# adaLN attention, mixer and MLP on one core: matmul order in the MLP and in attention, PSUM pools, and the hand-over to mixing

## The chip, the cores and the metric

The kernel runs on one core of a Trainium2 chip. The metric is the device time of one execution in microseconds. The kernel before was timed three times: 1797.48, 1798.19 and 1798.49 us, median 1798.19. One further execution was profiled; it took 1793.53 us, and the trace, its page and all rows quoted below are of that one.

Engines are named as the profile names them: PE (matmuls; PEld is its weight load, which runs beside them), DVE (vector), ACT (scalar), POOL (GpSimd) and SP, whose queue issues nearly all DMAs. L12 is line 12 of the kernel.

## What is computed

One transformer block over 2048 rows of 576 features, with three stages. The conditioning vector c gives six vectors (sa, ca, ga, sb, cb, gb) by silu(c) times w_mod.

```
h  = layernorm(x) * (1 + ca) + sa
x  = x + ga * (attention(h) @ wo)             # 32 heads of 18, causal window of 256 rows
h  = layernorm(x) * (1 + cb) + sb
g  = gelu(layernorm(h) @ w1)                  # 576 x 576
x1 = h + shift(g) @ w2                        # four feature groups, shifted by +1, -1, +2, -2 rows
h2 = gelu(layernorm(x1) @ w3) @ w4            # 576 -> 4608 -> 576
x  = x + gb * (x1 + h2)
```

All of it is in 32-bit floats. The kernel splits each operand into a high and a low part that PE can multiply fast, and adds three products (high x high, high x low, low x high) in PSUM: a contraction over 576 features takes 14 matmuls, namely 3 for each of four chunks of 128, and 2 for the tail of 64.

## The kernel before

Rows are cut into 16 tiles of 128 and four blocks of 512; a block is the moving operand of most matmuls. Three phases follow each other.

**Attention** (`phase_a`, L161). It works through 32 units u, eight per row block: a unit is four heads of one row block. For a unit, `pack` (L431) loads Q and K from DRAM, where the Q and K products had been stored; `scores` (L446) makes 16 score tiles "sc" and takes each row's maximum on DVE; `attend` (L494) recomputes the transposed scores X in three PSUM banks for each head (L504), adds masks by matmuls with an identity (L513), takes the exponential on ACT (`ex`), multiplies by V (`av`, L534), transposes and divides (`ot`, `on`), and stores the result to `od` in DRAM (L555). The table `banks` (L491) lists, bank by bank, the pieces of X as (key tile, first query tile, width in tiles, place in the bank); `low` (L492) the masks as (which, place, width). Between these, the Q, K and V products of the next row block are played: `x_tr` (L328) transposes the normalized rows in five chunks k (PE, then ACT to a 32-bit buffer h, then POOL's high and DVE's low part) into the tile hT, and `qk_item` and `v_item` (L370, L412) are its 17 products of 14 matmuls. The window of a row block for these products, in units, is in `win` (L700). When the last window is over, `s4a` (L703) does the output product, the residual, the two norms and the modulation for the first 12 row tiles, beside the last attention units; it stores rows to DRAM as xp, hbd and xnd.

**Mixing** (`phase_b`, L923). Rows come back from xnd, are transposed (`split9`, L67: four 128-wide transposes "pa" and a tail "pb" per row tile, a high part by ACT, L74 and L80, and a low part by DVE, L75 and L81) into tiles xnT of 512 rows, and go through W1 (`w1c`, products pg, L986) and gelu into G; shifted, they go through W2 (L1037). The last four row tiles of the output product (`s4`) run here too. `w2t` (L936) loads the 64 rows of W2 that make its tail chunk, splits them and moves the low part by DMA.

**MLP** (`phase_c`, L1168). 36 units: two halves of the rows (blk) times 18 pairs of 128 hidden features (fg). In a unit, `up` makes four items of 14 matmuls 128x512 (L1231) with a gelu each; POOL and ACT and DVE form sums and splits of the results (`after`, L1211). `down` takes a unit's results one unit later: seven combinations m times four row tiles i are 28 groups of three matmuls 128x288 (L1276), and each is added to an accumulator in SBUF by DVE (L1283). The seven combinations replace eight products of 2 x 2 blocks.

**What sets the order.** Every step is put on a list with a time number, in units, and `play` (L42) sorts the list: the numbers are no times on the chip, they are the order of the program. In attention and MLP the engines then run their instructions in that order; mixing is ordered by the framework's own scheduler. A step that needs a buffer waits until its last reader is done. PSUM has eight banks: in attention 3 "sc" (scores), 2 "st" (X), and one each of "tr" (transposes), "av" and "mm" (products); in the other phases 3 "w1", 2 "w2", 2 "tr" and one "mm", from a pool of its own. In SBUF, "L" is one buffer that holds hT in turn, then 8 rows of `s4a` (s4rows), then xnT0, xnT3 and LNT3; "L2" has three for the other xnT and LNT tiles.

Lines of importance for what follows: the spread of the parts of an up item, L1237, and the time of a down group, L1321.

```
ev += spread([part(2 * k, 2 * k + 2) for k in range(7)], t, t + 0.25)      # L1237
t = t0 + 0.005 + 0.965 * (n + 0.5) / 28                                    # L1321
```

## Time and profile before

| what | us |
|---|---|
| timed, median of 3 | 1798.19 |
| profiled execution | 1793.53 |
| its span, first to last instruction | 1791.7 |
| start and first products | 0 to 66 |
| attention with products | 66 to 507 |
| attention with `s4a` | 507 to 707 |
| between attention and mixing | 707 to 722 |
| mixing | 722 to about 890 |
| MLP | about 890 to 1791 |

The stages were read off the trace: attention's last copy stands at 707.05 and the first mixing product at 722.13. A row of busy time by stage has the window, its length, and for each engine the busy microseconds and the instructions; then the granted clock of PE as a share of full speed, the busy share of the DMA engines, and GB/s. A timeline row has start, duration, engine, line, operation, output and inputs, shape of the stationary and moving operands, and how many such instructions in a row; in brackets, the time that the engine had stood idle and what ended that. Matmuls overlap, so a row's duration is longer than the distance to the next row's start; what a group costs PE is that distance. A row of a waits view has who waited, for what, how many microseconds in all, how often, and the longest.

### The profile page before, as it was taken

To read this page: it belongs to the slowest core of one execution; us is meant where nothing else is said; L and a number is where in the kernel's file an instruction comes from. 1 tells how busy PE (TensorE), PEld (TensorE's weight loads), DVE (VectorE), ACT (ScalarE), POOL (GpSimd) and SP (SyncE) were. 2 spreads that over 40 slices of the span, in tenths; PEclk is the share of its full clock that TensorE was granted. 3 is DMA by queue.
4 is the path that set the end of the run, shared out by engine and by line. 5 is a ranking of instruction groups with operands and counts; after the bars stand their busy time and mean duration, and the time that the engine had idled before them with its cause. 6 is when DMAs were issued, how large, how long until landed. Compare 5 with 4: busy or idle time off the path is not lost.

```text
span 1791.7 us, 31913 instructions
## 1 busy us (share of the span) xinstructions
PE 1712.6 (96%) x11100; PEld 1431.1 (80%) x11100; DVE 1227.2 (68%) x3050; ACT 713.7 (40%) x1310; POOL 839.5 (47%) x829
## 2 busy tenths in 40 slices
PE   8899999999988897999999999999999999999998
PEld 5767777777866675788988888888888888888887
DVE  3564665575566764676777778887777777777777
ACT  3354454464455555444243344443332222222221
POOL 7332332321135553011188888888875333333335
PEclk9999999999999999899999999999999999999999
DMA  7554454434356654543455565556655444444442
GB/s 214 165 161 139 126 160 133 116 116 119 105 120 179 205 152 134 170 129 108 139 196 179 202 213 199 188 187 204 208 203 191 141 149 145 161 140 164 141 133 90
DMA packets 161544, 283.41 MB, mean 158 GB/s; under 512 B 38756, under 2 KB 77668, under 8 KB 161384
## 3 DMA queue, kind: packets, MB, share of 16 engines
q1 hardware_dynamic: 161064, 280.85, 49.3%
q8 instruction: 88, 1.44, 0.3%
q14 instruction: 72, 0.59, 0.1%
q10 hardware_dynamic: 320, 0.52, 0.1%
HBM read 168.86 MB, written 111.78 MB: 157 GB/s over the span
## 4 chain that ended last, share of the span: by engine, by line
PE 75%; DVE 7%; POOL 6%; DMA 5%; issue 4%; ACT 2%; SPq 1%; DVEq 0%; POOLq 0%; ACTq 0%
PE p L1231 21%; PE p L1276 19%; PE qk L365 6%; PE av L534 4%; PE X L504 4%; PE sc L457 4%; PE v L365 3%; PE X L513 3%; PE w L1037 2%; PE pg L986 2%; PE po L752 2%; DMA r<-in_B_w_dram 1%; POOL g L1204 1%; POOL c L1132 1%; DMA wm<-in_w_mod_dram 1%
## 5 line engine op out<-in xcount | busy, mean ns | idle before, releaser
L1231 PE MATMUL p<-LNT,W 128*128 128x512 f32 x2016 | 628.7, 399 | 0.0
L1276 PEld LDWEIGHTS p<-W,G 128*128 128x128 f32 x3036 | 505.2, 189 | 116.7 <-DVE accA L1283 14.7
L1276 PE MATMUL p<-W,G 128*128 128x288 f32 x3036 | 559.9, 296 | 16.7 <-DVE accA L1283 7.7
L464 DVE CUSTOM_DVE_ANT_0 sc<-sc,mask 128x384 f32<-128x384 f32 (+2 forms) x512 | 271.4, 542 | 199.7 <-PE sc L457 197.3
L1283 DVE TENSOR_TENSOR accA<-p,accA 128x288 f32<-128x288 f32 x672 | 293.1, 453 | 134.9 <-PE p L1276 131.9
L1231 PEld LDWEIGHTS p<-LNT,W 128*128 128x128 f32 x2016 | 327.4, 188 | 5.4
L1204 POOL TENSOR_TENSOR g<-g,g 128x512 f32<-128x512 f32 x140 | 204.9, 1463 | 245.6 <-ACT g L1235 240.3
L523 ACT ACTIVATE P<-X 128x512 f32<-128x512 f32 (+2 forms) x384 | 216.8, 570 | 230.7 <-PE X L513 224.9
L1199 DVE TENSOR_TENSOR G<-g,G 128x512 fp32r<-128x512 f32 x249 | 247.1, 992 | 28.2 <-ACT G L1196 27.7
L1196 ACT CAST G<-g 128x512 fp32r<-128x512 f32 x249 | 154.7, 621 | 225.5 <-POOL g L1204 222.0
L1235 ACT ACTIVATE g<-p 128x512 f32<-128x512 f32 x144 | 85.7, 595 | 360.3 <-DVE accA L1283 211.3
L457 PE MATMUL sc<-K,Q 108*128 108x384 f32 (+2 forms) x512 | 191.1, 381 | 6.1 <-DMA k0d<-qe 2.7
L504 PE MATMUL X<-Q,K 110*128 110x128 f32 (+2 forms) x704 | 163.1, 306 | 4.4 <-ACT P L523 3.8
L365 PE MATMUL qk<-hT,Wc 128*128 128x512 f32 x504 | 160.3, 417 | 2.7 <-ACT qe L386 1.3
L504 PEld LDWEIGHTS X<-Q,K 110*128 110x128 f32 x704 | 123.6, 191 | 30.0 <-issue 9.5
L390 POOL CAST qe<-qe 128x512 fp32r<-128x512 f32 x36 | 22.1, 615 | 255.8 <-ACT qe L386 245.7
L1283 DVE TENSOR_TENSOR accB<-p,accB 128x288 f32<-128x288 f32 x268 | 114.0, 448 | 26.9 <-PE p L1276 24.9
L513 PE MATMUL X<-maskb,identb 128*128 128x256 bf16 (+1 forms) x640 | 120.5, 254 | 0.0
L457 PEld LDWEIGHTS sc<-K,Q 108*128 108x128 f32 x512 | 96.9, 192 | 28.5 <-issue 11.8
L365 PEld LDWEIGHTS qk<-hT,Wc 128*128 128x128 f32 x504 | 87.7, 194 | 17.6 <-issue 5.1
L534 PE MATMUL av<-P,V 128*32 128x384 f32 (+2 forms) x1408 | 99.6, 395 | 0.0
L365 PE MATMUL v<-Wv,hT 128*128 128x288 f32 x448 | 82.9, 307 | 3.8 <-ACT qe L386 2.9
(902 smaller groups left out, 2087.1 us busy)
## 6 DMA issues: line engine op xcount, KB each, us to landing
w4d<-W SPq DMA_DIRECT2D x55, 576.0 KB
W<-w4d SPq DMA_DIRECT2D x55, 576.0 KB
w3d<-W SPq DMA_DIRECT2D x36, 640.0 KB
W<-w3d SPq DMA_DIRECT2D x36, 640.0 KB
K<-k0d SPq DMA_DIRECT2D x96, 108.0 KB
r<-in_B_w_dram SPq DMA_DIRECT2D x36, 288.0 KB
Q<-q0d SPq DMA_DIRECT2D x128, 72.0 KB
K<-k1d SPq DMA_DIRECT2D x48, 108.0 KB
```

The lines of the kernel that those rows point to most:

```text
L365: nc.tensor.matmul(pm, pl()[i][0], pl()[i][1], start=(i == 0), stop=(i == 13))
L457: nc.tensor.matmul(sc[:, lo:], q[0:2 * R3, h, i * P:(i + 1) * P], k[0:2 * R3, h // 2, i * P + lo:(i + 3) * P], start=True, stop=True)
L464: nc.vector.tensor_tensor_reduce(out=sc[:, lo:], in0=sc[:, lo:], in1=mask[:, lo:], scale=1.0, scalar=-3e38, op0=ALU.add, op1=ALU.max, accu ...
L504: nc.tensor.matmul(x[:, p0 * P:(p0 + w) * P], k[0:2 * R3 + 2, h // 2, (kb + 2) * P:(kb + 3) * P], q[0:2 * R3 + 2, h, q0 * P:(q0 + w) * P], ...
L513: nc.tensor.matmul(x[:, p0 * P:(p0 + w) * P], self.identb, m, start=False, stop=(n == len(ms) - 1))
L523: nc.scalar.activation(pt[:, c0:c1, h % 2, :], x[:, c0 * P:c1 * P].rearrange("p (a b) -> p a b", b=P), AF.Exp, scale=SCALE)
L534: nc.tensor.matmul(abox[0][32 * h:32 * h + 32, q0 * P:(q0 + w) * P], v[:, hh * VA:hh * VA + 32], Pt[b, h // 2][:, p0:p0 + w, h % 2, :], st ...
L1199: nc.vector.tensor_tensor(out=sp[m][:, 1], in0=src(), in1=sp[m][:, 0].bitcast(F32), op=sub)
L1204: nc.gpsimd.tensor_tensor(out=g[o] if o in g else gt(o), in0=g[a], in1=g[b], op=op)
L1231: nc.tensor.matmul(box["p"], box["l"][i][1], box["l"][i][0], start=(i == 0), stop=(i == 13))
L1276: nc.tensor.matmul(po, a, b, start=(n == 0), stop=(n == len(seq) - 1))
L1283: nc.vector.tensor_tensor(out=acc[m, i], in0=po, in1=acc[m, i], op=ALU.add)
```

## The change

Seven edits, which move, add and resize steps; no matmul, cast or transfer is taken away.

1. **MLP order.** The 14 matmuls of an up item are played as two runs of seven, where they were seven pairs. The down groups stand in bursts of three or four between these runs, where they were spread evenly.
2. **One PSUM pool** "ps" for all phases, with the attention's tags: "w1" is taken from the three "sc" banks, "w2" from the two "st" banks, and the transposes of mixing and half of the down groups ("t2") take "tr" and "av" in turn.
3. **Mixing's first tiles.** Only LNT0 still uses the buffer "L"; xnT0, xnT3 and LNT3 go to "L2". V, Q and K get a pool of their own. The first four row tiles are transposed in the "w1" and "w2" banks. `w2t` is placed at 0.2, after the first mixing steps, where it stood at -0.9.
4. **Order in an attention bank.** Bank 0 begins with its 384-wide piece, and its masks are in the other order.
5. **Prologue.** The first weights' loads are issued after the conditioning step: a 1x1 memset on DVE stands ahead of them. Some of the first products take the "av" bank in place of "mm", and the fourth Q/K product is a little earlier.
6. **Row blocks.** The five chunks of `x_tr` follow each other at 0.08 units from 0.4 before the window, where it was 0.16 from 0.8 before. Their 32-bit buffer is a pair of two in "qe". The windows in `win` are longer.
7. **Tail of attention.** Tiles of `s4a` start at 0.75 + 0.70 t after the window, where it was 0.85 + 0.72 t, and take the tile "oT" later.

The diff, cut to its core:

```diff
-    def split9(self, row, L, cs, name):
+    def bank(self, shape, kind, name, dt=F32):
+        tag = {"w1": "sc", "w2": "st"}.get(kind, kind)
+        if kind == "t2":
+            tag = ("tr", "av")[next(self.turn) % 2]
+        return self.ps.tile(shape, dt, tag=tag, name=name, bufs={"sc": 3, "st": 2}.get(tag, 1))
+
+    def split9(self, row, L, cs, name, kind="t2"):
...
-            pa = self.ps.tile([P, KC, P], F32, tag="tr", name=name + "pa", bufs=self.pb["tr"])
+            pa = self.bank([P, KC, P], kind, name + "pa")
...
+        self.ps = self.pool(stack, "ps", space=PSUM)
+        self.turn = itertools.count()
...
-            self.ps = self.pool(st, "psA", space=PSUM)
+            kv = self.pool(st, "kV")
...
+                    if c == 0:
+                        nc.vector.memset(raws[c][0:1, 0, 0:1], 0.0)
...
-                    if g:
-                        h = kp.tile([P, 512], F32, tag="h32", name=f"h{g}_{k}", bufs=1)
-                    else:
-                        if k % 2 == 0:
-                            h0["t"] = kp.tile([P, 2, 512], F32, tag="qe", name=f"h{g}_{k}", bufs=2)
-                        h = h0["t"][:, k % 2, :]
+                    if k % 2 == 0:
+                        h0["t"] = kp.tile([P, 2, 512], F32, tag="qe", name=f"h{g}_{k}", bufs=2)
+                    h = h0["t"][:, k % 2, :]
...
-            banks = [[(3, 3, 1, 0), (0, 0, 3, 1)], [(1, 1, 3, 0), (-2, 0, 1, 3)], [(-1, 0, 2, 0), (2, 2, 2, 2)]]
-            low = [((1, 0, 2), (0, 3, 1)), ((1, 0, 1), (0, 2, 2)), ((None, 1, 2),)]
+            banks = [[(0, 0, 3, 1), (3, 3, 1, 0)], [(1, 1, 3, 0), (-2, 0, 1, 3)], [(-1, 0, 2, 0), (2, 2, 2, 2)]]
+            low = [((0, 3, 1), (1, 0, 2)), ((1, 0, 1), (0, 2, 2)), ((None, 1, 2),)]
...
-                    ev += x_tr(g, k, w0 - 0.8 + 0.16 * k)
+                    ev += x_tr(g, k, w0 - 0.4 + 0.08 * k)
...
-                t0 = w1 + 0.85 + 0.72 * t
+                t0 = w1 + 0.75 + 0.7 * t
...
-    win = {1: (2.95, 9.0), 2: (9.8, 15.8), 3: (16.6, 22.4)}
+    win = {1: (2.9, 9.25), 2: (9.7, 16.1), 3: (16.55, 22.73)}
...
-                if not tail:
-                    box["T"] = gp.tile([P, 2 * KC + 1, P], F32R, tag="oT", name=f"oT{t}", bufs=1)
...
+                if not tail:
+                    box["T"] = gp.tile([P, 2 * KC + 1, P], F32R, tag="oT", name=f"oT{t}", bufs=1)
...
-    def ltile(self, name, first):
-        if first:
+    def ltile(self, name):
+        if name == "LNT0":
...
-            tra, trb = self.split9(lambda: box["x"], lambda: xnT[g], slice((t % 4) * P, (t % 4 + 1) * P), f"xnT{t}")
+            tra, trb = self.split9(lambda: box["x"], lambda: xnT[g], slice((t % 4) * P, (t % 4 + 1) * P), f"xnT{t}", ("w1" if t < 3 else "w2") if g == 0 else "t2")
...
-        ev = [(-1.5, begin), (-0.9, w2t), (3.05, first)]
+        ev = [(-1.5, begin), (0.2, w2t), (3.05, first)]
...
-                ev += spread([part(2 * k, 2 * k + 2) for k in range(7)], t, t + 0.25)
+                ev += [(t, part(0, 7)), (t + 0.125, part(7, 14))]
...
-                    po = box[m, i] = ps.tile([P, DH2], F32, tag=("w2", "tr")[next(cnt) % 2], name=f"p4{nm}_{m}_{i}", bufs=2)
+                    po = box[m, i] = ps([P, DH2], ("w2", "t2")[next(cnt) % 2], f"p4{nm}_{m}_{i}")
...
-                t = t0 + 0.005 + 0.965 * (n + 0.5) / 28
+                t = t0 + (2 * n + 1) // 7 * 0.125 + 0.06 + 0.005 * (n % 7)
...

```

What the numbers do to the order of the program shows at three places. A row has the line, the operation, output and inputs by the program's names, the output's columns (or rows and columns), and how often it stands in a row.

**PE in the MLP**, at the start of unit 5 of the first half (p3 is an up item: half, unit, item; p4 a down group: half, unit, combination, row tile; x3 is one group). Before:

```order
L1231 MATMUL p30_5_0_12231<-LNT0_9806,W30_5_0_12124 128x512 x2
L1276 MATMUL p40_4_1_0_12234<-W40_4_0_12003,G10_4_12030 128x288 x3
L1231 MATMUL p30_5_0_12231<-LNT0_9806,W30_5_0_12124 128x512 x2
L1276 MATMUL p40_4_1_1_12244<-W40_4_0_12003,G10_4_12030 128x288 x3
L1231 MATMUL p30_5_0_12231<-LNT0_9806,W30_5_0_12124 128x512 x2
L1276 MATMUL p40_4_1_2_12252<-W40_4_0_12003,G10_4_12030 128x288 x3
L1231 MATMUL p30_5_0_12231<-LNT0_9806,W30_5_0_12124 128x512 x2
L1276 MATMUL p40_4_1_3_12262<-W40_4_0_12003,G10_4_12030 128x288 x3
L1276 MATMUL p40_4_2_0_12271<-W40_4_3_12053,G20_4_12107 128x288 x3
L1231 MATMUL p30_5_0_12231<-LNT0_9806,W30_5_0_12124 128x512 x2
```

Of the change:

```order
L1236 MATMUL p30_5_0_12224<-LNT0_9801,W30_5_0_12120 128x512 x7
L1281 MATMUL p40_4_1_0_12237<-W40_4_0_11994,G10_4_12025 128x288 x3
L1281 MATMUL p40_4_1_1_12241<-W40_4_0_11994,G10_4_12025 128x288 x3
L1281 MATMUL p40_4_1_2_12246<-W40_4_0_11994,G10_4_12025 128x288 x3
L1236 MATMUL p30_5_0_12224<-LNT0_9801,W30_5_0_12120 128x512 x7
L1281 MATMUL p40_4_1_3_12268<-W40_4_0_11994,G10_4_12025 128x288 x3
L1281 MATMUL p40_4_2_0_12276<-W40_4_3_12049,G20_4_12102 128x288 x3
L1281 MATMUL p40_4_2_1_12282<-W40_4_3_12049,G20_4_12102 128x288 x3
L1281 MATMUL p40_4_2_2_12289<-W40_4_3_12049,G20_4_12102 128x288 x3
```

Pairs of ups alternated with one group, rarely two; now seven ups, three groups, seven ups, four groups.

**PE at the hand-over** from the last attention unit (X31, av31, oT31) to mixing (xnT0 to xnT4 are row tiles, pa the four wide transposes and pb the tail; pg is the first W1 product). Before:

```order
L534 MATMUL av31_8794<-P31_2_0_8831,V4_159 32x256 x2
L534 MATMUL av31_8794<-P31_2_2_8852,V4_159 32x256 x2
L545 MATMUL oT31_8881<-ident_68,avs31_8875 128x128 x4
L73 MATMUL xnT0pa_9061<-ident_68,xn0_9052 128x128 x4
L79 MATMUL xnT0pb_9068<-ident_68,xn0_9052 64x128
L73 MATMUL xnT1pa_9072<-ident_68,xn1_9054 128x128 x4
L79 MATMUL xnT1pb_9079<-ident_68,xn1_9054 64x128
L73 MATMUL xnT2pa_9083<-ident_68,xn2_9056 128x128 x4
L79 MATMUL xnT2pb_9090<-ident_68,xn2_9056 64x128
L73 MATMUL xnT3pa_9094<-ident_68,xn3_9058 128x128 x4
L79 MATMUL xnT3pb_9101<-ident_68,xn3_9058 64x128
L986 MATMUL pg0_4_9128<-xnT0_9060,W14_6430 128x512 x2
```

Of the change, where xnT0pa, xnT1pa and xnT2pa stand ahead of X31's last pieces already:

```order
L540 MATMUL av31_8789<-P31_2_2_8850,V1_159 32x256
L79 MATMUL xnT3pa_9073<-ident_71,xn3_9037 128x128 x4
L540 MATMUL av31_8789<-P31_2_2_8850,V1_159 32x256
L540 MATMUL av31_8789<-P31_2_0_8826,V4_162 32x256 x2
L540 MATMUL av31_8789<-P31_2_2_8850,V4_162 32x256 x2
L551 MATMUL oT31_8879<-ident_71,avs31_8873 128x128 x4
L85 MATMUL xnT1pb_9058<-ident_71,xn1_9033 64x128
L991 MATMUL pg0_4_9107<-xnT0_9039,W14_6496 128x512 x2
L991 MATMUL pg0_0_9159<-xnT0_9039,W10_6658 128x512
L85 MATMUL xnT0pb_9047<-ident_71,xn0_9031 64x128
L85 MATMUL xnT3pb_9080<-ident_71,xn3_9037 64x128
```

The wide transposes of tiles 0 to 3 moved ahead of the last transposes oT31, and the first products ahead of the tails.

**ACT at the same place** (avs31 is the copy of the last attention result, s4rows with c11rs the norm of row tile 11). Before:

```order
L539 COPY avs31_8875<-av31_8794 128x512
L133 ACTIVATE s4rows_6175<-s4rows_6175,c11rs_8877 128x576
L941 CAST W2t_9031<-rw2t_9036 128x576
L74 CAST xnT0_9060<-xnT0pa_9061 128x4x128
L80 CAST xnT0_9060<-xnT0pb_9068 64x128
L74 CAST xnT0_9060<-xnT1pa_9072 128x4x128
L80 CAST xnT0_9060<-xnT1pb_9079 64x128
L74 CAST xnT0_9060<-xnT2pa_9083 128x4x128
```

Of the change:

```order
L545 COPY avs31_8873<-av31_8789 128x512
L80 CAST xnT0_9039<-xnT0pa_9040 128x4x128
L80 CAST xnT0_9039<-xnT1pa_9051 128x4x128
L86 CAST xnT0_9039<-xnT1pb_9058 64x128
L80 CAST xnT0_9039<-xnT2pa_9062 128x4x128
L80 CAST xnT0_9039<-xnT3pa_9073 128x4x128
L139 ACTIVATE s4rows_6234<-s4rows_6234,c11rs_8875 128x576
L86 CAST xnT0_9039<-xnT0pb_9047 64x128
L86 CAST xnT0_9039<-xnT3pb_9080 64x128
```

W2t's cast is gone from its place ahead of xnT0's, and the casts of tiles 0 to 3 follow the copy directly, ahead of the norm.

**PE at the first row block's change** (X2_0 is bank 0 of unit 2, hT1 the transposed rows of block 1, sc the scores of the next unit). Before:

```order
L337 MATMUL hT1_2_1322<-ident_68,x4_908 128x128
L337 MATMUL hT1_2_1322<-ident_68,x5_936 128x128
L337 MATMUL hT1_2_1322<-ident_68,x6_960 128x128
L337 MATMUL hT1_2_1322<-ident_68,x7_983 128x128
L504 MATMUL X2_0_1_1330<-Q2_167,K2_170 128x128
L504 MATMUL X2_0_1_1330<-Q2_167,K2_170 128x384
L513 LDWEIGHTS identb_173
L513 MATMUL X2_0_1_1330<-maskb_172,identb_173 128x256
L513 LDWEIGHTS identb_173
L513 MATMUL X2_0_1_1330<-maskb_172,identb_173 128x128
L457 MATMUL sc3_2_0_1337<-K0_168,Q0_165 128x384
```

Of the change:

```order
L346 MATMUL hT1_1_1330<-ident_71,x4_901 128x128
L346 MATMUL hT1_1_1330<-ident_71,x5_926 128x128
L346 MATMUL hT1_1_1330<-ident_71,x6_947 128x128
L346 MATMUL hT1_1_1330<-ident_71,x7_974 128x128
L510 MATMUL X2_0_2_1335<-Q2_170,K2_173 128x384
L510 MATMUL X2_0_2_1335<-Q2_170,K2_173 128x128
L519 LDWEIGHTS identb_176
L519 MATMUL X2_0_2_1335<-maskb_175,identb_176 128x128
L519 LDWEIGHTS identb_176
L519 MATMUL X2_0_2_1335<-maskb_175,identb_176 128x256
L463 MATMUL sc3_2_1_1342<-K0_171,Q0_168 128x384
```

The piece of 384 columns now stands first in the bank, and the chunks of hT follow each other after one X group, where two stood between.

48 lines of the change are left out of this document (23 added, 25 removed).

## Prediction

> **What bounds the kernel now.** I read the page first, then busy time by stage, then the chain.
>
> ```profile
> PE 1712.6 (96%) x11100; PEld 1431.1 (80%) x11100; DVE 1227.2 (68%) x3050; ACT 713.7 (40%) x1310; POOL 839.5 (47%) x829
> PE 75%; DVE 7%; POOL 6%; DMA 5%; issue 4%; ACT 2%; SPq 1%; DVEq 0%; POOLq 0%; ACTq 0%
> 66.00:507.00 441.00, 428.50 (x3257) 326.65 (x3257) 259.26 (x884) 216.02 (x401) 118.38 (x140) 0.99 0.44 128
> 507.00:707.00 200.00, 178.39 (x1513) 137.30 (x1513) 130.99 (x444) 111.69 (x203) 96.12 (x123) 0.99 0.58 165
> 707.00:722.00 15.00, 5.40 (x25) 3.54 (x24) 4.90 (x14) 4.85 (x11) 0.78 (x2) 0.68 0.75 222
> 890.00:1340.00 450.00, 439.34 (x2494) 383.26 (x2494) 353.81 (x655) 182.49 (x339) 379.14 (x316) 1.00 0.59 199
> 1340.00:1791.00 451.00, 442.35 (x2545) 393.37 (x2543) 331.10 (x648) 116.30 (x193) 178.67 (x136) 0.99 0.43 145
> ```
>
> The stage rows give length, then busy PE, PEld, DVE, ACT and POOL with their counts, and the granted clock. PE is 97 to 98% busy in attention and in both MLP halves, 89% in the attention tail with the output projection, and 36% in the fifteen microseconds between attention and mixing. So two kinds of saving count: matmuls that follow each other more closely where PE is full, and the idle time at that one boundary. Transfers and POOL matter only where PE waits for them.
>
> The diff removes no matmul, cast or transfer; it adds one 1x1 DVE memset. Everything below is order, buffers and waits. I sum against the profiled execution, 1793.53 us (1.8 us of it outside the span of 1791.7), and move the sum unchanged to the timed median, 1798.19, which lies 4.7 us higher.
>
> **MLP: runs of seven, bursts of three or four.** A unit interleaves 56 up matmuls (L1231) with 28 down groups of three (L1276); 35 of the 36 units hold both. The timeline of PE gives start, duration, instruction and count.
>
> ```profile
> 1500.86 0.64 PE L1231 MATMUL p<-LNT,W 128*128 128x512 f32 x2
> 1501.33 0.56 PE L1276 MATMUL p<-W,G 128*128 128x288 f32 x3
> 1501.72 0.64 PE L1231 MATMUL p<-LNT,W 128*128 128x512 f32 x2
> ...
> 1502.59 1.09 PE L1231 MATMUL p<-LNT,W 128*128 128x512 f32 x4
> 1503.52 0.56 PE L1276 MATMUL p<-W,G 128*128 128x288 f32 x3
> ...
> 1506.12 0.96 PE L1276 MATMUL p<-W,G 128*128 128x288 f32 x6
> 1506.91 0.63 PE L1231 MATMUL p<-LNT,W 128*128 128x512 f32 x2
> ```
>
> From start to start, two ups take 0.47 us, one triple 0.39, four ups in a row 0.93, six downs 0.79. So a longer run of ups saves about 0.01 us per pair after its first, and a longer run of downs saves nothing; within the rows' rounding it may lose 0.01 per triple. Even the run of four, which is two different banks, shows no cost for changing bank: what costs is the change of shape. Eight runs of seven have 20 further pairs in place of a break each: -0.2 to -0.3 us, plus 0 to 0.2 for the downs. I take -0.23 us a unit, times 35 = **-8 us**. Ends: -11, and above zero if the bursts stall PE:
>
> ```profile
> L1283 DVE TENSOR_TENSOR accA<-p,accA 128x288 f32<-128x288 f32 x672 | 293.1, 453 | 134.9 <-PE p L1276 131.9
> PE p L1276 <- DVE accA L1283: 7.7, 11, 2.5
> PE p L1276 <- DVE accB L1283: 5.8, 9, 1.3
> ```
>
> An eviction takes 0.453 us, a down group 0.39. Four groups in a row leave DVE 4 x 0.453 - 4 x 0.39 = 0.25 us behind, and the next seven ups (about 1.6 us) are its time to catch up. Four banks serve the downs, as before, so a bank's next writer comes after a gap of about 2.8 us (three groups and seven ups) instead of 3.1 (three triples and four pairs). DVE has the G splits of POOL's sums in the same queue; two of them now stand directly behind each other after the first burst. Waits for evictions were 13.5 us in the two main rows; by their doubling the term ends at +5.
>
> **Boundary 707 to 722.** In order: the copy of the last attention result, the last division, its store, G's memset, the first cast of xnT0, its low part, the next transposes, and the tail of tile 4.
>
> ```profile
> 707.05 0.58 ACT L539 COPY avs<-av 128x512 f32<-128x512 f32 x1 [1.14 <-PE av L534]
> 708.71 0.46 DVE L553 TENSOR_TENSOR o<-oT,rc 128x288 f32<-128x288 f32 x1
> 709.20 0.37 SPq L555 DMA_DIRECT2D od<-o  x1
> 711.59 0.11 DVE L973 MEMSET G<- 128x20 f32 x2 [2.42 <-DMA od<-o]
> 713.94 0.58 ACT L74 CAST xnT<-xnT0pa 128x512 fp32r<-128x512 f32 x1 [1.81 <-DMA xnd<-s4rows]
> 714.56 0.69 DVE L75 TENSOR_TENSOR xnT<-xnT0pa,xnT 128x512 fp32r<-128x512 f32 x1 [1.64 <-ACT xnT L74]
> 715.28 0.28 DVE L81 TENSOR_TENSOR xnT<-xnT0pb,xnT 64x128 fp32r<-64x128 f32 x1
> 715.31 1.12 PE L73 MATMUL xnT1pa<-ident,xn 128*128 128x128 f32 x4 [5.30 <-DVE xnT L75]
> 728.09 0.27 PE L79 MATMUL xnT4pb<-ident,xn 128*64 128x128 f32 x1
> 715.00:720.00 5.00, 2.66 (x10) 1.75 (x10) 1.92 (x5) 1.48 (x4) 0.00 (x0) 0.50 0.92 281
> ```
>
> Two stores hold the first cast: W2t's cast stands ahead of it on ACT and waits for od's store, and xnT0 takes the "L" buffer, whose old rows leave in xnd's. Then tiles 1 to 3 go through one bank in a loop of 2.5 us each. The change cuts all three: W2t is placed later, xnT0 gets L2, and the first four tiles have four banks and are transposed before attention's last products. In the new ACT order four casts and a tail follow the copy: 707.63 + 4 x 0.58 + about 0.3 = 710.2, when the first product can start. DVE has four wide low parts, the division and five short steps: from 708.2, 4 x 0.69 + 0.46 + 5 x 0.28 gives 712.6, and ACT's norm of row tile 11 stands ahead of three tails. About a dozen 512-wide matmuls at 0.23 and tile 4's four transposes stand between that low part and xnT4pb: 712.6 + 3.2 = 715.8, against 728.1. So **-12 us**; ends -14, and -5 if a store gates the first products after all. What is late next is od's store. On DVE the division now has two low parts around it, and on SP the store stands behind two loads (gb, and xn6, whose row buffer comes free with xnT0pb on PE, about 711); 2.4 us from issue to the memset's end of waiting puts G's memset and the gelu behind it at 713.4, while PE has products of the first two groups until about 715. So it is covered by some 2 us; each microsecond beyond costs one. W2t's eight loads, its cast and its four stores go behind those of row tiles 12 and 13 on SP, ACT and DVE; they hold nothing there that PE waits for, and W2t's own first product comes in the second mixing step, after five groups of 14.
>
> The granted clock is 0.50 in the five microseconds quoted; the sum has it at full. In the new order PE idles twice, about 1.8 and 1.7 us; were the dozen matmuls to run at half clock, 2.8 us of the 12 would be lost. [...]
>
> **Order within an attention bank (L491).** Bank 0 of each head (first rows) begins with its 128-wide piece and masks 256 then 128; bank 1 (last rows) begins with the 384-wide one and masks 128 then 256.
>
> ```profile
> 286.93 0.45 PE L504 MATMUL X<-Q,K 110*128 110x128 f32 x2
> 287.22 0.34 PE L513 MATMUL X<-maskb,identb 128*128 128x256 bf16 x2
> 287.37 0.65 PE L365 MATMUL v<-Wv,hT 128*128 128x288 f32 x3
> ...
> 289.00 0.40 PE L504 MATMUL X<-Q,K 110*128 110x384 f32 x2
> 289.24 0.34 PE L513 MATMUL X<-maskb,identb 128*128 128x128 bf16 x2
> 289.34 0.42 PE L457 MATMUL sc<-K,Q 108*128 108x384 f32 x1
> ...
> L504 PE MATMUL X<-Q,K 110*128 110x128 f32 (+2 forms) x704 | 163.1, 306 | 4.4 <-ACT P L523 3.8
> ```
>
> Same sizes, 0.44 us against 0.34 from the first piece to the next instruction. The change gives bank 0 the order of bank 1: 0.10 us x 4 heads x 32 units = 12.8 us of PE time. Three quarters of the units lie where PE is 97% busy, the rest at 89%; I count about 85%: **-11 us**. Ends: -13, and -3 if waits for ACT's exp take most of it.
>
> **Row blocks and prologue.** The five hT chunks of a block now come every 0.08 units in place of 0.16 (about 1 us for 2), and the block's first products sooner after them; the single 32-bit buffer, through which the chunks went one by one, becomes two pairs.
>
> ```profile
> L337 PE MATMUL hT<-ident,x x20: 270/272/327, 104.5 to 114.7; 128*128 128x128 f32 x16, 128*64 128x128 f32 x4
> L347 ACT ACTIVATE h<-hT,sa,ca x5: 774/778/778, 105.2 to 115.4; 128x512 f32<-128x512 f32 x4, 64x512 f32<-64x512 f32 x1
> 95.00:125.00 30.00, 28.03 (x215) 19.93 (x213) 20.69 (x79) 18.72 (x36) 10.52 (x16) 1.00 0.49 148
> ```
>
> PE is idle 2 us of these 30; a better spread of the products over wider windows can save perhaps 1 us a block. Against it: all chunks use one "tr" bank, whose next writer waits for 0.78 us of ACT plus an exp ahead of it, while PE has about an X group, a score and a product in between. A stall of 0.7 us x 4 x 3 blocks is +8. I take **0**, ends -3 and +8.
>
> ```profile
> L365 PE MATMUL v<-Wv,hT 128*128 128x288 f32 x448 | 82.9, 307 | 3.8 <-ACT qe L386 2.9
> PE sc L457 <- DMA k0d<-qe: 2.7, 1, 2.7
> 29.00:49.00 20.00, 16.59 (x84) 13.30 (x84) 4.07 (x6) 7.12 (x15) 19.34 (x15) 1.00 0.49 148
> ```
>
> In the prologue the products alternate two banks, so PE's waits for copies (3.8 us before v, nearly all there) go; but POOL, 19.34 of 20 us busy, feeds k0d, for which PE waits 2.7 us later: the wait grows by what is saved. **-0.5**, ends -3 and +1.5 (the weights' loads, held behind the memset, come later).
>
> At nothing I cost the rest. One PSUM pool in place of two lets mixing's banks be taken before attention's last ones are free; that is in the boundary's term. In the tail (507 to 707) PE idles 21 us around the one "mm" bank and the row passes; tiles start 0.70 units apart in place of 0.72, twelve times, with the same waits: 0, ends -2 and +2. V, Q and K in a pool of their own move addresses only.
>
> Sum: -8 - 12 - 11 + 0 - 0.5 = **-31.5**: 1762 us profiled, 1766.7 timed, so **1767**.
>
> **Rivals.** *Evictions bind the MLP, slower* (4%): if the 0.25 us that a burst of four leaves on DVE is not caught up, and the splits ahead make it the same for three, PE waits 0.25 us x 8 bursts x 35 units = +70 us: 1767 + 70 = 1837. It turns slower than before above 0.13 us a burst (280 x 0.13 = 36); DVE is busy 354 of 450 us in the first half, which speaks for it, but has 21% in hand, which speaks against. [...] *The bursts cost what the runs give* (14%): waits double, 1780. *The X saving becomes waits for exp* (12%): -3 in place of -11, 1775; the page's row has 3.8 us of such waits now, which speaks against. *The boundary only moves the wait*, so that the change doesn't do what it says (8%): od's store gates the first gelu and through its bank PE, 5 us of 12 remain, 1774. *hT stalls* (9%): 1775. *Several of these at once* (3%): no change, 1796. *As forecast* (50%): 1759 to 1773.
>
> **How the numbers follow.** Faster by over 0.2% (3.6 us, about what a measurement of this kernel can tell from no change) holds all cases but two: 0.93, same 0.03, slower 0.04. The low end of the range takes all good ends (MLP -3, X -2, boundary -2, hT -3, prologue -2.5, tail -2: 1752); the high end takes the MLP's doubled waits and the hT stalls together (1767 + 13 + 8 = 1788). Range 1752 to 1788; outside it lie the last 7% and the odd pair of rivals.
>
> **What would show it.** Right: seven ups take about 1.62 us (0.47 + 2.5 x 0.46); bank-0 groups take 0.34 us; xnT4pb starts about 9 us after the last attention copy (before 21), with a clock near 1 behind it. Wrong: more than 30 us of PE waits for accA or accB; idle PE before hT above 3 us a block; a wait for od's store inherited by PE at the first gelu; attention as long as before with more idle time behind exp.

## The result, and the profile after

The changed kernel takes 1787.68 us (median of 4, 1784.61 to 1789.77) against 1797.84 of the kernel before in the same comparison: a ratio of 0.9944, interval 0.9926 to 0.9961. It is 10 us faster. The forecast was 31 us, so the time lies at the very end of the stated range, and the gain is a third of the one foretold.

The page of the changed kernel and its busy time by stage, in the columns used above:

```profile
span 1785.4 us, 31972 instructions
PE 1693.3 (95%) x11100; PEld 1435.8 (80%) x11100; DVE 1217.8 (68%) x3051; ACT 715.3 (40%) x1310; POOL 831.1 (47%) x829
PE 63%; POOL 11%; DVE 10%; DMA 6%; issue 6%; ACT 2%; SPq 1%; DVEq 0%; POOLq 0%; ACTq 0%
...
707.00:722.00 15.00, 13.90 (x74) 11.65 (x75) 7.85 (x17) 8.67 (x17) 0.00 (x0) 0.92 0.68 200
...
890.00:1340.00 450.00, 422.14 (x2425) 374.45 (x2424) 359.12 (x643) 175.24 (x326) 366.52 (x307) 1.00 0.57 195
1340.00:1785.00 445.00, 434.65 (x2543) 393.02 (x2541) 310.98 (x648) 116.82 (x191) 171.82 (x136) 0.99 0.46 147
```

The third line has the shares of the chain of work that ended last: PE's fell from 75% to 63%, and POOL's and DVE's rose from 6 and 7% to 11 and 10%. In the first half of the MLP PE is busy 422 of 450 us, where it was 439. So something there waits that did not before. To see where the time went, the two traces are laid beside each other by ACT instructions that both have: the copy of each attention unit's result (32 of them), the first gelu of mixing, and the first gelu of each MLP unit.

| stretch | before, us | after, us | difference |
|---|---|---|---|
| start to the copy of unit 0 | 93.1 | 93.9 | +0.8 |
| copy of unit 0 to unit 9 | 170.0 | 171.4 | +1.4 |
| copy of unit 9 to unit 10 | 23.0 | 32.7 | +9.7 |
| copy of unit 10 to unit 31 | 421.0 | 402.2 | -18.7 |
| last copy to the first gelu of mixing | 21.2 | 12.5 | -8.7 |
| to the first gelu of the MLP | 161.5 | 161.6 | +0.1 |
| MLP, 16 units of the first half | 398.2 | 412.7 | +14.5 |
| MLP, 15 units of the second half | 363.7 | 358.4 | -5.3 |

The MLP units that the table leaves out, at the change of halves and at the end, add -1.9 and +1.8. Two rows have the wrong sign and count for much, unit 10 and the first half of the MLP. Both show in what PE waited for, over the whole changed kernel (who, for what, us, times, longest):

```profile
PE p L1281 <- DVE accB L1288: 23.2, 24, 1.4
PE pm L595 <- POOL wm L589: 9.5, 2, 7.7
```

accB had 5.8 us before. One of these waits in the first half of the MLP, in the timeline of DVE and PE of the changed kernel:

```profile
1075.95 3.20 DVE L1204 TENSOR_TENSOR G<-g,G 128x512 fp32r<-128x512 f32 x2
...
1077.88 0.56 PE L1281 MATMUL p<-W,G 128*128 128x288 f32 x3
...
1079.08 0.44 DVE L1288 TENSOR_TENSOR accB<-p,accB 128x288 f32<-128x288 f32 x1
1079.45 2.26 DVE L1288 TENSOR_TENSOR accA<-p,accA 128x288 f32<-128x288 f32 x6
1079.57 1.25 PEld L1281 LDWEIGHTS p<-W,G 128*128 128x128 f32 x9 [1.38 <-DVE accB L1288]
1079.58 1.50 PE L1281 MATMUL p<-W,G 128*128 128x288 f32 x9 [1.14 <-DVE accB L1288]
```

Two G splits stand behind each other and take 3.20 us from the first one's start to the second one's end, without a wait in between. The eviction that PE needs comes at 1079.08. PE starts a burst at 1077.88, does one group, and stands for 1.14 us until a bank is free: it wanted the bank 2.49 us after the pair's start (1079.58 - 1.14 - 1075.95), and the eviction ended 3.57 us after it. The groups of DVE by line show how long a split is in either half (busy us, mean ns of one, idle before it and who ended that), first from 915 to 1315 us, then from 1360 to 1740; and, of the second stretch, the shortest, median and longest in ns:

```profile
L1204 DVE TENSOR_TENSOR G<-g,G 128x512 fp32r<-128x512 f32 x110 | 132.6, 1216 | 31.6 <-ACT G L1201 29.3
```

```profile
L1204 DVE TENSOR_TENSOR G<-g,G 128x512 fp32r<-128x512 f32 x113 | 91.5, 832 | 0.0
L1204 DVE TENSOR_TENSOR G<-g,G x113: 672/681/1921, 1359.4 to 1739.8; 128x512 fp32r<-128x512 f32 x113
```

The same instruction takes 0.68 us or up to 1.92. In the first half it is longer, and it waits 29.3 us in all for ACT's high parts. Each unit has two such pairs, some 4.3 us apart. With every PE gap over 0.25 us put to the pair that it follows, the 32 pairs of the first stretch fall into four kinds. The room is the time from the pair's start to the moment at which PE wants the bank that the first eviction behind the pair frees; the last column is the time to the end of that eviction.

| pairs | wait before the pair, us | the two splits together, us | PE gap behind, us | room, us | eviction ended after, us |
|---|---|---|---|---|---|
| 9, first of their unit | 0.2 to 0.3 | 2.9 | none | 3.9 | 3.3 |
| 9, second, behind those | none | 3.2 (one 3.7) | 0.7 (one 1.2) | 2.9 | 3.6 (one 4.1) |
| 7, first of their unit | 1.2 | 2.9 | 0.8 to 1.2 | 2.2 to 2.6 | 3.3 |
| 7, second, behind those | none | 3.2 | 1.1 | 2.5 | 3.6 |

These gaps are 21.8 of the 23.3 us: 6.9 in units where no pair waited for long, 14.9 in units where the first pair waited 1.2 us. So a long pair costs time without a wait, and more behind one. A gap is the eviction's end less the room, to within 0.1 us, in every row.

The other, in unit 10 of the attention, by POOL, PE and SP:

```profile
280.50 0.75 POOL L587 TENSOR_SCALAR wm<-wm,silu 128x576 f32<-128x576 f32 x1 [8.56 <-DMA wm<-in_w_mod_dram]
...
282.70 1.27 POOL L400 TENSOR_TENSOR qe<-qe 128x512 fp32r<-128x512 f32 x1
...
284.00 0.32 SPq L412 DMA_DIRECT2D k1d<-qe  x1
284.85 0.50 SPq L580 DMA_DIRECT2D wm<-in_w_mod_dram  x1
...
288.68 1.39 POOL L589 TENSOR_TENSOR wm<-wm 64x576 f32<-64x576 f32 x1
...
290.12 1.33 PE L595 MATMUL pm<-wm,ones 128*128 128x288 f32 x2 [7.71 <-POOL wm L589]
```

pm is the broadcast of one of the modulation vectors (`modvec`), which POOL sums over five loads. POOL stood 8.56 us for the fourth load. Behind it in POOL's queue stood the split of a Q/K product (qe, L400), whose store SP issued at 284.00, ahead of the fifth load at 284.85. So POOL waited for SP, SP for POOL, and PE for both.

### The profile page after: what moved, and what is told of

It reads as the page before. It is cut to its first block, busy times and chain, and to the rows that moved or that the text cites. A ratio compares the mean times of both kernels' runs of the same rounds, so it can differ in the third digit from the quotient of the medians.

```text
span 1785.4 us, 31972 instructions
## 1 busy us (share of the span) xinstructions
PE 1693.3 (95%) x11100; PEld 1435.8 (80%) x11100; DVE 1217.8 (68%) x3051; ACT 715.3 (40%) x1310; POOL 831.1 (47%) x829
## 4 chain that ended last, share of the span: by engine, by line
PE 63%; POOL 11%; DVE 10%; DMA 6%; issue 6%; ACT 2%; SPq 1%; DVEq 0%; POOLq 0%; ACTq 0%
PE p L1281 14%; PE p L1236 14%; PE qk L371 5%; PE av L540 4%; PE X L510 4%; PE sc L463 4%; POOL g L1209 4%; PE pg L991 3%; PE X L519 3%; PE v L371 3%; PE w L1042 3%; DVE G L1204 2%; PE po L759 2%; DMA r<-in_B_w_dram 2%; DVE accB L1288 2%
## 5 line engine op out<-in xcount | busy, mean ns | idle before, releaser
L1236 PE MATMUL p<-LNT,W 128*128 128x512 f32 x2016 | 508.1, 392 | 0.0
L1281 PE MATMUL p<-W,G 128*128 128x288 f32 x3036 | 456.5, 297 | 35.9 <-DVE accB L1288 23.2
L1281 PEld LDWEIGHTS p<-W,G 128*128 128x128 f32 x3036 | 434.4, 189 | 67.7 <-DVE accB L1288 30.3
L1236 PEld LDWEIGHTS p<-LNT,W 128*128 128x128 f32 x2016 | 364.4, 189 | 60.2
L1288 DVE TENSOR_TENSOR accA<-p,accA 128x288 f32<-128x288 f32 x672 | 272.1, 452 | 125.3 <-PE p L1281 124.8
L1209 POOL TENSOR_TENSOR g<-g,g 128x512 f32<-128x512 f32 x140 | 193.1, 1379 | 237.9 <-ACT g L1240 232.5
L510 PE MATMUL X<-Q,K 110*128 110x384 f32 (+1 forms) x704 | 157.1, 298 | 4.6 <-ACT P L529 3.3
L1288 DVE TENSOR_TENSOR accB<-p,accB 128x288 f32<-128x288 f32 x268 | 109.1, 450 | 27.4 <-PE p L1281 27.0
```

What stands on the lines that cost most here:

```text
L510: nc.tensor.matmul(x[:, p0 * P:(p0 + w) * P], k[0:2 * R3 + 2, h // 2, (kb + 2) * P:(kb + 3) * P], q[0:2 * R3 + 2, h, q0 * P:(q0 + w) * P], ...
L1209: nc.gpsimd.tensor_tensor(out=g[o] if o in g else gt(o), in0=g[a], in1=g[b], op=op)
L1236: nc.tensor.matmul(box["p"], box["l"][i][1], box["l"][i][0], start=(i == 0), stop=(i == 13))
L1281: nc.tensor.matmul(po, a, b, start=(n == 0), stop=(n == len(seq) - 1))
L1288: nc.vector.tensor_tensor(out=acc[m, i], in0=po, in1=acc[m, i], op=ALU.add)
```

## The experiments

Each ratio is against the kernel before on the same chip, with its 95% interval; 0.001 is 1.8 us. The kernel before had medians from 1794 to 1798 us on the chips used, so runs on different chips are better compared by their ratios than by their medians. In the expectations, D is the theory that evictions are late in DVE's queue, W that PE stands behind a broadcast.

**The MLP order taken back** (e1):

```diff
-                ev += [(t, part(0, 7)), (t + 0.125, part(7, 14))]
+                ev += spread([part(2 * k, 2 * k + 2) for k in range(7)], t, t + 0.25)
...
-                t = t0 + (2 * n + 1) // 7 * 0.125 + 0.06 + 0.005 * (n % 7)
+                t = t0 + 0.005 + 0.965 * (n + 0.5) / 28
```

> The changed kernel with the MLP order of before (ups in pairs, down groups spread evenly); all else as changed. Theory D (DVE's queue: in the first half of the MLP two G splits stand directly behind each other after a burst, wait for POOL's sums through ACT, and hold the evictions behind them, so PE waits): the first half returns from 25.8 us a unit to 24.9 (14 us gained), the second from 23.9 to 24.25 (7 us lost), together about 7 us faster than the changed kernel, near 1780. Theory B (the stalls come from the banks of the shared pool, with tr and av one buffer each for the down groups, and not from the order): the first half stays near 25.8 us a unit and the time is 1788 or more.

Measured: 0.9914 (0.9891 to 0.9937), 1778.82 us. Without the MLP edit the kernel is 5 us faster than with it by the ratios (0.9944 - 0.9914 = 0.0030, though the two intervals overlap), 9 by the medians. The 16 first-half units take 397.3 us again, the 15 of the second 363.7, as before. PE's wait for accB is back at its old size:

```profile
PE p L1281 <- DVE accB L1288: 6.0, 10, 1.3
```

**Runs and bursts in the second half only** (e2): the new numbers where `blk` is 1, the old ones where it is 0.

> The changed kernel with runs of seven and bursts in the second half of the MLP only; the first half has the order of before. Theory D: 14 us faster than the changed kernel, near 1773, with first-half units of 24.9 us and second-half units of 23.9. Theory B: no gain in the first half, near 1788.

Measured: 0.9876 (0.9851 to 0.9900), 1773.36 us. The first half takes 396.5 us, the second 358.4: the gain of the second half without the loss of the first.

**The MLP order of the change alone, in the kernel before** (e3): edit 1 with the old PSUM pools.

> The kernel before with the MLP order of the change alone (two runs of seven, bursts of three and four), its own PSUM pools kept. Theory D: slower than before by about 7 us, near 1805: +14 in the first half, where PE waits over 25 us for accB, and -7 in the second. Theory B: the banks are those of before, so both halves gain: -8 to -11, near 1789.

Measured: 1.0068 (1.0044 to 1.0091), 1807.0 us, 12 us slower than before. In the trace the first half takes 411.5 us and the second 358.4. The banks are the old ones and the waits are there, so the shared pool is not their cause:

```profile
PE p L1276 <- DVE accB L1283: 22.5, 24, 1.4
```

**The order within attention's bank 0 alone, in the kernel before** (e4): the two tables `banks` and `low` of edit 4.

> The kernel before with the order within attention's bank 0 alone (384-wide piece first, masks 128 then 256). If the PE time saved converts: each bank-0 group 0.34 us in place of 0.45, and attention ends 11 to 13 us earlier, near 1786. If waits for exp or DVE take its place: the groups are as short, but attention ends at most 3 to 5 us earlier, near 1794.

Measured: 0.9965 (0.9953 to 0.9977), 1787.55 us: 6 us by the ratio, 4 to 8 by its interval. In the trace the stretch from the first to the last copy is 603.4 us against 614.0 before, 10.6 less. The groups are as short as foretold; one of this kernel, in its timeline of PE, takes 0.33 us from its first piece to the next instruction:

```profile
283.48 0.40 PE L504 MATMUL X<-Q,K 110*128 110x384 f32 x2
283.72 0.34 PE L513 MATMUL X<-maskb,identb 128*128 128x128 bf16 x2
283.81 0.65 PE L365 MATMUL v<-Wv,hT 128*128 128x288 f32 x3
```

So the saving in PE time becomes time; waits for exp did not take its place.

**G splits apart** (e5): both halves in runs and bursts, but the low parts of the splits later, so that one at most stands between two bursts.

```diff
-                    return split((1, 2, 7, 4)[n], src(n), t + 0.03)
+                    return split((1, 2, 7, 4)[n], src(n), t + 0.03, 0.19 if n < 2 else 0.035)
...
-                return e + [x for m, k, d in ((5, 2, 0.105), (6, 0, 0.16), (3, 1, 0.215)) for x in split(m, src(k), t + d)]
+                return e + [x for m, k, d, l in ((5, 2, 0.105, 0.035), (6, 0, 0.16, 0.08), (3, 1, 0.215, 0.12)) for x in split(m, src(k), t + d, l)]
```

> The changed kernel with runs and bursts in both halves of the MLP, but with the low parts of G6, G3, G1 and G2 played later, so that one of them stands between two bursts on DVE and no two directly behind each other. Theory D (evictions are late because two splits that wait stand ahead of them): PE's waits for accB in the first half fall from 23 us to under 8, its units from 25.8 us to at most 24.9, and the kernel is 14 to 18 us faster than the changed one, 1770 to 1774. If a burst of four by itself is too much for DVE in the first half (0.25 us of lag with DVE 80% busy), units stay above 25.4 us and the time above 1782.

Measured: 0.9891 (0.9870 to 0.9912), 1777.36 us, 10 us faster than the changed kernel. The first half takes 404.4 us: 8 of its 14.5 us are won, not all. accB's waits are gone, but new ones stand for accA, and DVE's own waits in the first half show a reason, a scaling of loaded weights (r, L1128) that waits for its load, in the same queue:

```profile
PE p L1281 <- DVE accA L1288: 13.4, 12, 2.6
...
DVE r L1128 <- DMA r<-in_B_w_dram: 29.9, 10, 5.8
```

No two splits follow each other on DVE from 905 to 1335 us any more. All 13 PE gaps over 0.25 us there, 14.5 us together, stand behind a scaling that had waited 3.9 to 5.8 us. (These loads had 18.6 us of DVE's waiting in the changed kernel, where all but 1.5 us of such gaps stand behind the pairs.) So the pairs' gaps are gone, and this wait, which cost little before, took their place in part. Either way the eviction came late because of what stood ahead of it in DVE's queue.

**Broadcasts later** (e6): the two broadcasts of each modulation vector on PE, and what follows them, 0.6 units later.

```diff
-                    return [(0.0, f), (0.02, e)]
+                    return [(0.6, f), (0.62, e)]
```

> The changed kernel with the broadcasts of the modulation vectors on PE (pm) 0.6 units later. In the changed kernel PE waits 9.5 us for POOL's wm, 7.7 of them at once in unit 10. Theory W (PE's in-order queue stands behind a broadcast whose sum on POOL waits for a load that is late on SP): the wait goes, attention ends 5 to 8 us earlier, near 1781. Rival: POOL and SP hold each other up there anyway (a Q/K split behind the sum, the next load behind its store), and PE waits for Q or K instead: less than 2 us gained, near 1787.

Measured: 0.9873 (0.9856 to 0.9890), 1774.04 us, 13 us faster than the changed kernel, more than either theory gave. PE does not wait for wm any more; its largest wait in attention is one of the prologue's:

```profile
PE sc L463 <- DMA k0d<-qe: 4.6, 1, 4.6
```

Unit 10 takes 19.8 us in place of 32.7, and the stretch from the first copy to the last 590.8 us in place of 606.3. The wait itself was 9.5 us; why 13 to 15 go with it was not followed up.

**Edit 6 taken back in the changed kernel** (e7): chunks at 0.16 units, single buffer, old windows.

> The changed kernel with edit 6 taken back: chunks of the transposed rows 0.16 units apart from 0.8 before the window, one 32-bit buffer, windows as before. If edit 6 costs (denser chunks and the moved windows meet the wm chain): faster than the changed kernel by 3 to 9 us, near 1782, and unit 10 loses under 3 us against before where the changed kernel loses 10. If edit 6 gains or is even, as predicted: 1787 to 1791.

Measured: 0.9963 (0.9948 to 0.9978), 1789.15 us, 1.5 us slower by the medians and 3.4 by the ratios than the changed kernel; these intervals overlap. Unit 10 loses nothing against before (22.5 us against 23.0), so edit 6 brings that wait about; without it the attention's tail loses instead (units 24 and 25 together are 9.5 us longer than before), so neither theory held as a whole.

**Edit 3 taken back in the changed kernel** (e8):

```diff
-        if name == "LNT0":
+        if name in ("xnT0", "xnT3", "LNT3"):
...
-            tra, trb = self.split9(lambda: box["x"], lambda: xnT[g], slice((t % 4) * P, (t % 4 + 1) * P), f"xnT{t}", ("w1" if t < 3 else "w2") if g == 0 else "t2")
+            tra, trb = self.split9(lambda: box["x"], lambda: xnT[g], slice((t % 4) * P, (t % 4 + 1) * P), f"xnT{t}", "t2")
...
-        ev = [(-1.5, begin), (0.2, w2t), (3.05, first)]
+        ev = [(-1.5, begin), (-0.9, w2t), (3.05, first)]
```

> The changed kernel with edit 3 taken back: xnT0, xnT3 and LNT3 in the buffer L, LNT0 in L2, W2t at its place of before, and the first tiles' transposes in tr and av; the single PSUM pool stays. If the boundary's gain is of these buffers: the first mixing product starts again over 14 us after the last attention copy, and the time is 8 to 10 us above the changed kernel, near 1797. If it is of the single pool: within 2 us of the changed kernel.

Measured: 1.0003 (0.9987 to 1.0018), 1796.03 us: the whole of what the changed kernel gains goes, 10.6 us by the ratios. Both stores hold ACT again, in this kernel's timeline:

```profile
698.09 0.58 ACT L545 COPY avs<-av 128x512 f32<-128x512 f32 x1 [1.14 <-PE av L540]
704.50 0.67 ACT L946 CAST W2t<-rw2t 128x576 fp32r<-128x576 f32 x1 [2.40 <-DMA od<-o]
706.77 0.58 ACT L80 CAST xnT<-xnT0pa 128x512 fp32r<-128x512 f32 x1 [1.60 <-DMA xnd<-s4rows]
721.37 0.60 ACT L993 ACTIVATE gf<-pg 128x512 f32<-128x512 f32 x1 [1.56 <-PE pg L991]
```

From the last copy to the first gelu it is 23.3 us, where the changed kernel has 12.5. The single pool without edit 3 gains nothing here. Edit 3 has three parts, the buffers, W2t's place and the banks of the first tiles; they were taken back together, so how much each is worth stays open.

**Second-half runs with late broadcasts** (e9): e2 and e6 together in the changed kernel.

> The changed kernel with runs of seven and bursts in the second half of the MLP only, and the broadcasts of the modulation vectors 0.6 units later. If the two losses are separate (the evictions in the first half, 14 us; the broadcast in unit 10 and what follows, 13 us): 1787.7 - 14 - 13 = 1760 to 1762. If the earlier hand-over only shows another wait: 1766 or more.

Measured: 0.9793 (0.9768 to 0.9817), 1759.11 us. By the ratios e2 gains 0.0068 and e6 0.0071 on the changed kernel, and this run 0.0151: the two losses are separate and add up.

**Short runs in the first half** (e10): as e9, but the first half has runs of four and three ups and bursts of two groups, with one group ahead of each new item.

```diff
-                ev += [(t, part(0, 7)), (t + 0.125, part(7, 14))]
+                ev += [(t, part(0, 7)), (t + 0.125, part(7, 14))] if blk else [(t + 0.0625 * k, part(a, b)) for k, (a, b) in enumerate(((0, 4), (4, 7), (7, 11), (11, 14)))]
...
-                t = t0 + (2 * n + 1) // 7 * 0.125 + 0.06 + 0.005 * (n % 7)
+                t = t0 + (2 * n + 1) // 7 * 0.125 + 0.06 + 0.005 * (n % 7) if blk else t0 + (n // 7 * 4 + n % 7 // 2) * 0.0625 + 0.03 + 0.005 * (n % 7 % 2)
```

> As the combination of second-half runs and late broadcasts, with runs of four and three ups and bursts of two down groups (one before each new item) in the first half of the MLP. Theory D: one G split between two bursts, and a lag of at most 0.12 us a burst, so nothing waits and the shorter alternation gains 0.15 us a unit there: 2 to 3 us faster than that combination, near 1758. If the first half is held by POOL's sums and DVE as such: no gain, near 1761, or a loss of 3 and more.

Measured: 0.9753 (0.9733 to 0.9772), 1753.16 us, the fastest of the study: 34 us below the changed kernel and 45 below the one before, both by the medians. The first half takes 392.1 us (before 398.2, with runs of seven 412.7), and PE's waits for evictions there are the smallest of the runs:

```profile
PE p L1281 <- DVE accA L1288: 4.1, 5, 2.1
PE p L1281 <- DVE accB L1288: 1.7, 2, 1.0
```

Against e9 the gain is 7 us, by the ratios and by the first half of the traces (392.1 against 399.3), where 2 to 3 were expected. PE's idle time in these 16 units is 5 of it (1.5 us in place of 6.6).

**Late broadcasts in the kernel before** (e11): the edit of e6 alone.

> The kernel before with the broadcasts of the modulation vectors 0.6 units later, nothing else. If the loss at the broadcast is made by the change's new windows: the kernel before waits only 3.3 us for wm, so at most 2 to 4 us gained, ratio to before 0.998 to 0.999. If the wait is as much a loss of the kernel before: over 8 us gained, ratio under 0.9955.

Measured: 0.9959 (0.9947 to 0.9971), 1790.12 us: 7 us, between the two expectations. The kernel before lost time at its broadcasts too; the change made the loss about twice as large.

**Edit 6 alone in the kernel before** (e12):

> The kernel before with edit 6 alone (chunks of the transposed rows at 0.08 units, their buffer pairs, the longer windows). If the windows bring the broadcast's chain into collision: unit 10 loses 5 to 10 us against before, PE waits 6 us and more for wm, and part of it is won back by fuller windows, ratio to before 0.999 to 1.003. If edit 6 by itself is harmless: unit 10 within 2 us of before, and a ratio of 0.995 to 0.999 by denser blocks.

Measured: 1.0009 (0.9995 to 1.0023), 1799.32 us: no difference. Unit 10 is 5.7 us longer than before, by the same wait,

```profile
PE pm L586 <- POOL wm L580: 5.8, 1, 5.8
```

and the units after it win that back, so that first to last copy is 614.8 us against 614.0.

**POOL kept busy in the second half** (e13): the changed kernel with five more instructions on POOL in each unit there. L says that the pair holds the evictions by the length of its splits, S that it does so by its wait for POOL's sums.

```diff
+            if blk and not plain:
+                ev += [(t0 + 1.22 + 0.06 * k, lambda: nc.gpsimd.tensor_tensor(out=self.row("fill")[:, 0:512], in0=gb[:, 0:512], in1=gb[:, 0:512], op=add)) for k in range(5)]
```

> The changed kernel with five more tensor_tensor instructions on POOL in each unit of the MLP's second half, which write a scratch row that nobody reads. In the second half no split waits for POOL's sums, and POOL was busy 172 of 445 us. Theory L (a split is long beside a busy POOL, 0.68 us when POOL is idle beside it and 1.24 in the middle when POOL is busy, and the pair of splits holds the evictions by its length): the mean split of the second half goes from 0.83 to 1.0 us or more, PE waits for accB there too, and a unit goes from 23.9 to 24.3 to 24.9 us, the whole is 6 to 15 us slower than the changed kernel. Theory S (the pair holds evictions by waiting for the sums): nothing in the second half waits for them, so a unit stays at 23.9 us and the whole within 2 us of the changed kernel.

Measured: 0.9970 (0.9957 to 0.9984), 1791.64 us, 4 us above the changed kernel by the medians, with intervals that overlap. The trace doesn't put these 4 us there: the 15 units take 358.4 us again. Of the 4.8 us by which the profiled span is longer, 1.7 lie ahead of the second half, 1.0 in the unit at its start and 2.1 behind the last gelu. But POOL's company did make the split longer, from 832 to 1070 ns in the mean, by the groups of DVE from 1360 to 1740 us:

```profile
L1204 DVE TENSOR_TENSOR G<-g,G 128x512 fp32r<-128x512 f32 x112 | 117.3, 1070 | 0.0
```

So L is right about the length and wrong about the price. Here a pair takes 2.1 to 2.5 us, the eviction behind it ends 2.5 to 2.9 us after the pair's start, and the room is 3.5 to 4.2 us for all but the first two pairs of the stretch. Those two have 2.5, and PE waits 0.41 us behind one of them.

**POOL relieved in the first half** (e14): the low parts of the MLP's weights that POOL makes are plain copies on ACT, so the subtraction is left out.

```diff
-        l = (nc.gpsimd if fg else nc.vector).tensor_tensor
+        l = (lambda out, in0, in1, op: nc.scalar.copy(out, in0)) if fg else nc.vector.tensor_tensor
```

> The changed kernel with POOL's low parts of the MLP weights made by a plain copy on ACT in place of the subtraction, which is left out of the computation. POOL's busy time in the first half falls by 100 us or more of 367, and ACT has as much more. Theory L: the mean split of the first half goes from 1.22 us to 1.0 or less, and a unit from 25.8 to 24.9 us or less: the whole 10 to 16 us faster than the changed kernel. Theory S: ACT, which makes the high parts that the splits wait for, is busier, so the waits stay or grow: a unit stays at 25.8 or gets longer.

Measured: 0.9802 (0.9777 to 0.9828), 1759.3 us, 28 us below the changed kernel by the medians, 25 by the ratios. The first half takes 384.7 us in place of 412.7, a unit 24.0. Busy time from 900 to 1260 us, of the changed kernel and then of this one, and this one's group of splits there:

```profile
900.00:1260.00 360.00, 340.58 (x1958) 302.52 (x1958) 290.51 (x518) 141.85 (x266) 298.33 (x250) 1.00 0.56 190
```

```profile
900.00:1260.00 360.00, 358.26 (x2086) 321.26 (x2086) 284.10 (x553) 202.25 (x403) 180.25 (x150) 1.00 0.60 203
```

```profile
L1204 DVE TENSOR_TENSOR G<-g,G 128x512 fp32r<-128x512 f32 x105 | 104.9, 1010 | 29.0 <-ACT G L1201 27.0
```

POOL is 118 us less busy and ACT 60 us more, and PE is busy 358 of 360 us, with 1.5 us of gaps over 0.25 us. DVE still waits 27.0 us for the high parts of its splits in these 360 us (29.3 in 400 in the changed kernel), but no pair has such a wait ahead of it any more. So both the long pairs and the waits ahead of them went, and this run doesn't part L from S; the table of the changed kernel does, where pairs without a wait cost time too.

Most pairs take 2.5 us or less now, but six take 3.6 us and hold nothing up. One of them, in this kernel's timeline:

```profile
1077.80 1.25 DVE L1288 TENSOR_TENSOR accB<-p,accB 128x288 f32<-128x288 f32 x3
1078.97 3.64 DVE L1204 TENSOR_TENSOR G<-g,G 128x512 fp32r<-128x512 f32 x2
1080.01 1.75 PE L1281 MATMUL p<-W,G 128*128 128x288 f32 x12
1082.54 1.54 DVE L1288 TENSOR_TENSOR accB<-p,accB 128x288 f32<-128x288 f32 x4
1083.19 1.35 PE L1281 MATMUL p<-W,G 128*128 128x288 f32 x9
```

The pair starts when all earlier evictions are done, 1.04 us ahead of a burst of four, which has four free banks. PE wants the next bank at 1083.19, 4.22 us after the pair's start, and the first eviction behind the pair has ended by then (4.01 us after it). So a pair's length doesn't decide alone; it counts as well where the pair starts.

## Why the prediction was wrong

**MLP, forecast -8: wrong, and by far the largest error.** In the trace it is +14.5 - 5.3, or +9.1 with the units left out of the table, and by experiment +5 (e1) to +12 us (e3). The mechanism of the gain was right. In the second half seven ups take 1.60 to 1.62 us from start to start, as worked out, and a unit is 0.35 us shorter (5.3 over 15), a little above the -0.2 to -0.3 of the text:

```profile
1500.32 1.75 PE L1236 MATMUL p<-LNT,W 128*128 128x512 f32 x7
1501.92 1.35 PE L1281 MATMUL p<-W,G 128*128 128x288 f32 x9
1503.10 1.77 PE L1236 MATMUL p<-LNT,W 128*128 128x512 f32 x7
1504.72 1.75 PE L1281 MATMUL p<-W,G 128*128 128x288 f32 x12
```

The step that failed is "the next seven ups (about 1.6 us) are its time to catch up". It set the eviction's duration against the matmuls', as if DVE had nothing else in hand. The text itself names the two splits that now stand directly behind each other, and gives them no price. Beside a POOL that is busy for most of the half they take 2.9 to 3.2 us, and some wait 1.2 us for ACT ahead of that. The eviction behind them ends 3.3 to 3.6 us after the pair's start, where PE wants its bank after 2.2 to 2.9 us in 23 of 32 cases. Only the first half has it, since there POOL splits weights too: it was busy 379 of 450 us in the kernel before, and 179 in the second half. With POOL busier there (e13) a pair reaches 2.5 us, and nothing is lost in these units; with POOL relieved in the first half (e14) the loss is gone. The rival *the bursts cost what the runs give* had the mechanism and 14%; its price of +13 over the forecast was near, for the waits for evictions more than doubled (13.5 us in the two main rows to 30.3). That is also just past the prediction's own sign of being wrong, 30 us.

**Boundary, forecast -12: right, too large by a quarter.** -8.7 in the trace, -10.6 by e8. The order came out as foretold; the sizes from the changed kernel's timeline:

```profile
700.25 0.59 ACT L545 COPY avs<-av 128x512 f32<-128x512 f32 x1 [1.79 <-PE av L540]
...
703.67 1.12 PE L991 MATMUL pg<-xnT,W 128*128 128x512 f32 x3 [2.02 <-DVE xnT L81]
...
711.26 0.27 PE L85 MATMUL xnT4pb<-ident,xn 128*64 128x128 f32 x1
...
705.00:710.00 5.00, 4.81 (x17) 3.40 (x17) 2.39 (x8) 1.36 (x4) 0.00 (x0) 0.66 0.87 236
```

xnT4pb starts 11.0 us after the copy; the forecast was 9, before it was 21. Most of the 2 us can be the clock, by an estimate: it was granted at 0.66 between 705 and 710 with PE 4.81 of 5 us busy, which at full clock would be 3.2 us of work (4.81 x 0.66), if all of it goes with the clock as the 128x512 products did: 0.48 us each from start to start at 0.50 (three of pg from 706.73 to 708.17), 0.23 in the MLP's runs of seven at 1.00. The sum had the clock at full up to xnT4pb and named 2.8 us as the price of half; no run shows a full clock all the way there, and the changed kernel had 0.50 from 706 to 708. (Its sum for DVE, from 708.2, comes to 712.8 and not 712.6, which changes nothing.)

**Order in the bank, forecast -11: right in the mechanism; the size lies between the two measures.** It is 10.6 us by the trace of e4, one execution, but 6 by its ratio, with 4 to 8 in the interval. In the changed kernel this gain is mixed with edit 6: the differences of e4 and e12 from before, added, are +0.4, +5.3 and -15.6 us for the three attention rows from unit 0 on, where the changed kernel has +1.4, +9.7 and -18.7.

**Row blocks, forecast 0 with ends -3 and +8: right in size, by luck.** e12 has +1.6, e7 -3.4 by ratios, as a loss in unit 10 and a gain in later units nearly cancel. The stalls of the chunks in the "tr" bank, which were weighed, are small: PE waits 5.4 us for hT in all, 4.2 before. What was not weighed is that moved windows shift the stores of Q and K against the loads for the modulation vectors on SP and POOL. The waits view of before already had the row for it, 3.3 us of PE waiting for wm, and it was left out of the text.

**Prologue, forecast -0.5:** +0.8 in one trace each; kernels with an unchanged prologue (e3, e4, e11) show +1.2 to +1.5, so this says nothing.

Terms as measured by the ratios, +5 for the MLP, -11, -6 and -3, give -15, and the whole is -10; intervals of about 3 us each cover that. The chance of 93% for a gain was borne out. In the two traces the span is 6.3 us shorter, 25.2 short of the forecast. Of these, 17.1 are the MLP (+9.1 for -8), 3.3 the attention (-7.7 for -11), 3.3 the boundary (-8.7 for -12) and 1.3 the start.
